# Attention and a residual MLP on one core: the first weight kept on chip for four batches, and the second product of batches 0 and 1 moved behind that of 2 and 3

## The chip, the core and the metric

The kernel runs on one core of one Trainium2 chip. The metric is the device time of one execution in microseconds (us); lower is better. The kernel before the change takes 743.62 us, the median of three runs (743.61 to 744.68).

The core's engines are named as in the profile: PE (matrix products), PEld (its weight loads, beside PE), DVE (vector work), ACT (functions such as the exponential and ReLU), POOL (a small general engine that here mostly issues DMAs), SP (which only issues DMAs). Each engine executes its own instructions in the order in which the program puts them; a DMA issued from POOL or SP also waits in that order.

## The reference

```python
def reference(q, k, v, alpha1, beta1, w_tok, alpha2, beta2, w_ch1, w_ch2, lam):
    # q (8, 16, 384, 64); k, v (8, 4, 384, 64): four query heads share a key head
    s = q @ k.T / 8                                  # per head
    a = exp(s - max(s)); a = a / sum(a)
    x = concat_heads(a @ v)                          # (8, 384, 1024)
    u = x + lam * (w_tok @ (alpha1 * x + beta1))     # mixes the 384 tokens
    a2 = alpha2 * u + beta2
    h = relu(a2 @ w_ch1)                             # w_ch1 (1024, 4096): "W1"
    return u + lam * (h @ w_ch2)                     # w_ch2 (4096, 1024): "W2"
```

All inputs and the output are float32 in DRAM. The kernel computes in bf16 and gathers in float32.

## The kernel before

**Two parts for each batch.** The *side work* of a batch (function `side`, L230) is the attention, the token mixing and the turned `a2`. Its sixteen heads go in eight pairs `p`. A pair takes score products (L280), the exponentials on ACT (L289), the product with v and the row sums (`av_piece`, L307; four DVE instructions at L325, L328, L333, L335), the token product (`tok`, L341; two DVE instructions at L352, L356), a store of `u` into `out` from SP (`spill`, L243) and a turn of `a2` (a DMA transpose from SP, L367, or for a few pairs PE and ACT, `turn`, L429). The *main work* is `h = relu(a2 @ W1)` and `h @ W2`.

**Main work of batches 0 and 1** (`main`, L526). W1 is cut into 16 chunks of 256 columns (512 KB in bf16). A chunk is read with a cast by a POOL DMA (L185) into one of six slots (`RING`) and given up after use; batch 1 takes the chunks in the opposite order and reuses the last six. A chunk makes two tiles of h, each eight matmuls of 384 columns (L537; 385 for batch 0, whose extra column gives the bias `bias1`) and one ReLU, on ACT (L546) or DVE (L548). Four tiles of batch 0 are made early, at the end of batch 0's side work. W2 lies whole in `arena` (sixteen POOL loads, L189). The second product is six groups (`ch`, L575) of 32 matmuls of 512 columns for each batch. Each group is multiplied by `lam` on DVE and stored by SP (batch 0) or added into `out` by a POOL DMA (batch 1).

**Main work of batches 2 to 7** goes in pairs of batches (`pair`, L661). Both products use a scheme with seven products of half-size blocks in place of eight. The first product (L707) reads `opb` blocks (sums of turned `a2`, L591 to L593) and sums of W1 chunks (L626, L631), and writes five hidden blocks `hid[:, t, 0..4]`, which are derived from the four ReLU outputs; `hid` lies in `arena`. The second product (`C`, L757) is 7 x 3 x 16 = 336 matmuls of 512 columns per pair. Its right-hand operands are seven sets of W2 sums, made once by DVE from the raw W2 (`sum_w2`, L601), written by SP to the DRAM tiles `w2s`, and fetched by SP for every pair, 28 chunks of 512 KB, through the same six slots (`fetch`, L636). One `queue` (L653) gives each freed slot its next transfer.

**Order.** The program writes out the order by hand. `main` and `pair` are generators that yield after a few matmuls; a table `plan` tells which side work, loads and sums are emitted after which yield ("step"). Batch 1's side work lies in the second product of batch 0, batch 2's in the first product of batch 1, batch 3's in the second product of batch 1, and those of 4 and 5 together in the second product of the pair 2 and 3, and so on.

**Three small things that the change touches.** The vectors `lam`, `alpha1`, `beta1`, `alpha2` must lie on all partitions: SP loads rows of them (`load_row_set`, L886) and a DVE shuffle spreads them (`to_all`, L891). The PSUM banks of batch 0's side work (`lead_banks`) are given up and taken over by three double banks (`threes`). Exponentials can be put into a list `late` and emitted later.

Of the kernel before, what the change touches and what calls it, by code (L numbers as in the profile page):

```python
# [12 lines left out]
def kernel(  # L13
# [63 lines left out]
    w2 = arena.rearrange("p (t h d) -> p t h d", t=NH, h=2)  # L77
# [34 lines left out]
    w2s = [tc.dram_tile([P, NDT * CW * P], bf, name=f"w2s{i}") for i in range(SLOTS)]  # L112
    PLACE2 = {o: i for i, o in enumerate((1, 2, 6, 5, 3, 7, 4))}
# [4 lines left out]
    def row(nt):  # L118
        return nt % NH, nt // NH
# [61 lines left out]
    w1_slots, w1_free = {}, list(range(RING))  # L181

    def load_w1(c):
        w1_slots[c] = w1_free.pop(0)
        nc.gpsimd.dma_start(out=w1[:, w1_slots[c]], in_=w1src[:, :, c * CW * P:(c + 1) * CW * P])  # L185

    def load_w2(dw, r, h):
        cs = slice(dw * 512, (dw + 1) * 512)
        nc.gpsimd.dma_start(out=w2[:, 4 * r:4 * r + 4, h, cs], in_=w2src[:, h * NH + 4 * r:h * NH + 4 * r + 4, cs])  # L189
# [15 lines left out]

    def tp_ps(shape, tag="tp"):
        return bank(shape, tag, "tp", bf)

    late, exps = [], [0]
# [8 lines left out]
    def h_part(nts, dts):  # L218
        for nt in nts:
            if nt % 2 == 0 and nt not in early:  # L220
                t = bank([P, 2, 512], "sc", "h")
                early[nt], early[nt + 1] = t[:, 0], t[:, 1]
            for dt in dts:
                nc.tensor.matmul(out=early[nt][:, :S + 1], lhsT=w1[:, w1_slots[nt // CW], dt, nt % CW * P:(nt % CW + 1) * P],
                                 rhs=a2Ts[0][:, dt, :S + 1], start=(dt == 0), stop=(dt == NDT - 1))
# [4 lines left out]
    def side(b):  # L230
# [21 lines left out]
        def k_transpose(h0, n=2, tag="tp"):  # L252
            ps = tp_ps([P, n * NST, P], tag)
# [6 lines left out]
        def q_transpose(p, n=2, tag="tp", eng="DVE"):  # L260
# [3 lines left out]
            ps = bank([P, n * NST, P], tag, "tp", src.dtype)  # L264
# [7 lines left out]
        def scores(i, later=False):  # L272
# [11 lines left out]
            def exp():  # L284
# [6 lines left out]
                exps[0] = 0 if first else 2  # L291

            if later:
                late.append(exp)
            else:
                exp()
# [44 lines left out]
        def tok(p):  # L341
# [13 lines left out]
            a2s[p] = next_a2() if b > NPL + 1 else sb.tile([P, NST, P], bf, tag="a2", name="a2", bufs=2)  # L355
# [54 lines left out]
        def av(p):  # L410
            av_piece(p, 0)
            av_piece(p, 1)
            while late:
                late.pop(0)()
# [11 lines left out]
        def by_pe(p):  # L426
            return b % 2 and p >= (NP - 3 if b > NPL else NP - 1)

        def turn(p):  # L429
            ps = three()[:, 0].rearrange("p a b -> p (a b)").bitcast(bf)[:, :S].rearrange("p (a b) -> p a b", a=NST)  # L430
# [5 lines left out]
        if not first:  # L436


            turns = {}
            if b == 1:  # L440
                turns = {4: [(to_all, 3, 0, 0), (to_all, 3, 1, 1), (load_row_set, 1, 1, 0), (load_row_set, 2, 0, 1)],
                         8: [(k_transpose, 0)], 12: [(to_all, 1, 0, 2), (to_all, 1, 1, 0), (load_row_set, 2, 1, 0)],
                         16: [(scale_beta,)], 20: [(to_all, 2, 0, 1), (to_all, 2, 1, 0)],
                         24: [(q_transpose, 0, 2, "av")], 28: [(k_transpose, 2)]}
                for i in range(3):
                    turns[32 + 4 * i] = [(q_transpose, 2 + 2 * i, 2, "av")]
            if (b - NPL) // 2 > 0:
# [4 lines left out]

                for j in range(9):
                    put(4 * j, scores2, j)
                for p in range(NP):
                    put(4 * (p + 1) + 3, av, p)
                    put(4 * (p + 1) + 6, tok, p)
                    put(4 * (p + 1) + 8, flip, p)
                    if by_pe(p):
                        put(4 * (p + 1) + 8 + (p == NP - 3), turn, p)  # L460
                return turns, at
            return turns, {
# [5 lines left out]
                **{39 + 4 * i - i // 2 * 2: [(turn, p)] for i, p in enumerate((5, 6, 7)) if by_pe(p)}}  # L468
# [50 lines left out]
    def store(b, ms, dw, o):  # L519
        at = by_tok(out[b])[:, ms, dw * 512:(dw + 1) * 512]  # L520
        if b:
            nc.gpsimd.dma_start(out=at, in_=o, accum_op=ADD)  # L522
        else:
            nc.sync.dma_start(out=at, in_=o)

    def main(b):  # L526
# [3 lines left out]
        seq = order1[::-1 if b % 2 else 1]  # L530
        for i, c in enumerate(seq):
            for j in range(CW):
# [3 lines left out]
                for dt in range(0 if begun else NDT):  # L536
                    nc.tensor.matmul(out=ps[:, :n], lhsT=w1[:, w1_slots[c], dt, j * P:(j + 1) * P],  # L537
                                     rhs=a2T[:, dt, :n], start=(dt == 0), stop=(dt == NDT - 1))
                    if dt == 3:
                        yield 0  # L540
# [3 lines left out]
                exps[0] -= 1  # L544
                if nt % 2 == 0 and exps[0] < 0:
# [4 lines left out]
                yield 0  # L550
            if i + RING < NCH:
                w1_free.append(w1_slots.pop(c))
                load_w1(seq[i + RING])

            if b == 0 and i == NCH - RING:
                for dw, r, h in [(0, 1, 1)] + [(0, r, h) for r in (2, 3) for h in range(2)] + [
                        (1, r, h) for r in range(4) for h in range(2)]:
                    load_w2(dw, r, h)
                load_next(2)
        nts = [c * CW + j for c in seq for j in range(CW)]  # L560
        units = [(dw, ms) for dw in range(NDW) for ms in range(NST)]
        runs = [(k, 0, NNT) for k in range(len(units))]
        if b == 0:
            most = 3 * NNT // 4
            runs[:2] = [(k, lo, hi) for lo, hi in ((0, most), (most, NNT)) for k in range(2)]
        open_ps = {}
        for k, lo, hi in runs:
            dw, ms = units[k]
            cs = slice(dw * 512, (dw + 1) * 512)
            if lo == 0:  # L570
                open_ps[k] = bank([P, 512], "mm", "ch")
            ps = open_ps[k]
            for i in range(lo, hi):
                nt = nts[i]
                nc.tensor.matmul(out=ps, lhsT=hT[:, nt, ms * P:(ms + 1) * P],  # L575
                                 rhs=w2[:, row(nt)[0], row(nt)[1], cs], start=(i == 0), stop=(i == NNT - 1))
                if i % 4 == 3 and i < NNT - 1:
                    yield 1
            if hi < NNT:
                continue  # L580
            o = obuf[:, k % 2 * 512:(k % 2 + 1) * 512]
            nc.vector.tensor_tensor(out=o, in0=ps, in1=lam_t[:, cs], op=MUL)
            if b == 0:
                nc.vector.tensor_tensor(out=o, in0=o, in1=xs[0][:, ms, cs], op=ADD)
            store(b, ms, dw, o)
            yield 1
# [14 lines left out]
    def sum_w2(r, o, i=0):  # L601

        def get(m):
            return w2[:, 2 * r:2 * r + 2, int(m[0] == "2"), (m[1] == "2") * 512:(m[1] == "2") * 512 + 512]
# [17 lines left out]
    def sum_w1(g, o):  # L622
        a, c = w1[:, w1_slots[g]], w1[:, w1_slots[g + NCH // 2]]
# [9 lines left out]
    NB = (B - NPL) // 2  # L633
# [11 lines left out]
    def free(slot):  # L645
# [3 lines left out]
        if queue:  # L649
            f, *a = queue.pop(0)  # L650
            f(*a)

    queue = [m for i in range(NB) for m in [(load_w1, c) for c in order1[2 if i else RING:]]  # L653
             + [(fetch, i, n) for n in range(SLOTS - 2 if i + 1 < NB else SLOTS)] + [(load_w1, c) for c in order1[:2] if i + 1 < NB]]

# [365 lines left out]
```

## Time and profile before

| | |
|---|---|
| median of three runs | 743.62 us |
| the profiled execution | 745.27 us |
| its span, first to last instruction | 743.5 us |
| PE busy | 731.1 us, 98% of the span |
| DVE busy | 514.6 us, 69% |
| ACT busy | 319.3 us, 43% |
| DMA packets that POOL issued (software queue) | 65.8% of 16 engines' span |
| DMA packets that SP issued (hardware queue) | 42.3% |

The profile is one execution. A group of instructions is shown as: line, engine, operation, output <- inputs, shape, count | busy time, mean ns of one | idle time of the engine just before them and what ended it. The mean of a matmul is its latency; matmuls overlap, so busy time over count is nearer to what one takes. A table of windows gives the busy time of each engine in a stretch of the span, the number of instructions in brackets, then the granted PE clock, the DMA share and GB/s.

### The profile page before, as it was taken

The page shows a single profiled execution, that of the slowest core. Times are in us where ns is not written, and L with a number is a line of the kernel's source. Part 1 is how long each engine was busy: PE and PEld are TensorE (multiplying, and loading weights), DVE is VectorE, ACT ScalarE, POOL GpSimd, SP SyncE. Part 2 cuts the span into 40 slices and gives each one's busy share as a digit, 9 for nine tenths or more (in the row PEclk, how much of TensorE's full clock was granted, in tenths as well). Part 3 has the DMA queues.
Part 4 walks back from the last instruction along what each step waited for, and adds up shares of the span by engine and source line. Part 5 has one row for each costly group of instructions (what it writes and reads, how often), then busy time and mean ns, then how long its engine had stood idle before and what let it go on. Part 6 is the DMA issues. An engine that isn't in the chain of part 4 may idle for free.

```text
span 743.5 us, 14441 instructions
## 1 busy us (share of the span) xinstructions
PE 731.1 (98%) x5708; PEld 416.1 (56%) x5769; DVE 514.6 (69%) x998; ACT 319.3 (43%) x458; POOL 163.4 (22%) x211
## 2 busy tenths in 40 slices
PE   8999999999999999999999999999999999999997
PEld 5866555566555566645555566655555566654444
DVE  7763366567687889748778977747957987762354
ACT  7632431334332566653443366664334166660000
POOL 9434220420000232201003433210002331000011
PEclk9999999999999999999999999999999999999999
DMA  9999999999998999999979999998988998935976
GB/s 185 194 201 200 207 219 168 172 184 204 221 275 243 178 222 214 256 219 213 272 246 205 200 174 174 173 216 181 246 278 221 183 165 115 162 117 176 291 210 158
DMA packets 218017, 151.32 MB, mean 204 GB/s; under 512 B 88660, under 2 KB 197060, under 8 KB 217948
## 3 DMA queue, kind: packets, MB, share of 16 engines
q0 software_dynamic: 120304, 64.60, 65.8%
q1 hardware_dynamic: 97100, 85.39, 42.3%
q8 instruction: 45, 0.74, 0.4%
q10 hardware_dynamic: 544, 0.39, 0.2%
q14 instruction: 24, 0.20, 0.1%
HBM read 154.84 MB, written 38.27 MB: 260 GB/s over the span
## 4 chain that ended last, share of the span: by engine, by line
PE 85%; DMA 8%; POOL 2%; issue 2%; DVE 2%; POOLq 0%; DVEq 0%
PE C L757 29%; PE X L707 17%; PE Y L707 8%; PE ch L575 8%; PE h L537 7%; PE Z L707 4%; PE sc L280 4%; PE sc L345 3%; DMA ops<-a 3%; DMA w<-in_moe_w_ch_dram 2%; PE one L320 2%; DMA q_raw<-in_q_dram 2%; PE sc L320 1%; POOL w L185 1%; DMA rows<-in_moe_lam_dram 1%
## 5 line engine op out<-in xcount | busy, mean ns | idle before, releaser
L757 PE MATMUL C<-w,arena 128*128 128x512 bf16 (+2 forms) x949 | 219.9, 372 | 2.3
L289 ACT ACTIVATE es<-sc 128x1024 bf16<-128x1024 f32 x126 | 121.8, 1022 | 162.7 <-PE sc L280 158.6
L757 PEld LDWEIGHTS <-arena 128*128 128x128 bf16 x1040 | 93.7, 98 | 99.8 <-issue 7.6
L712 ACT ACTIVATE hT<-X,bias 128x384 f32<-128x384 f32 x144 | 83.7, 581 | 67.4 <-PE X L707 60.4
L707 PEld LDWEIGHTS <-w 128*128 128x128 bf16 x768 | 75.1, 98 | 50.3 <-issue 0.4
L185 POOL DMA_DIRECT2D w<-in_moe_w_ch_dram x68 | 62.4, 924 | 128.9 <-PE X L707 68.2
L575 PE MATMUL ch<-arena,hT 128*128 128x512 bf16 x366 | 87.9, 379 | 1.0 <-issue 0.3
L522 POOL DMA_DIRECT2D out_dram<-hT x33 | 29.3, 887 | 261.5 <-DVE hT L677 135.7
L537 PE MATMUL h<-ops,w 128*128 128x384 bf16 (+1 forms) x480 | 83.7, 327 | 1.9 <-DVE hT L548 0.9
L707 PEld LDWEIGHTS <-pad 128*128 128x128 bf16 x576 | 56.4, 98 | 37.2
L707 PE MATMUL X<-ops,w 128*128 128x384 bf16 x384 | 70.5, 326 | 0.0
L707 PE MATMUL X<-ops,pad 128*128 128x384 bf16 x384 | 70.3, 326 | 0.0
L537 PEld LDWEIGHTS <-w 128*128 128x128 bf16 x480 | 45.1, 98 | 32.3 <-issue 2.8
L575 PEld LDWEIGHTS <-hT 128*128 128x128 bf16 x384 | 34.7, 98 | 36.8 <-issue 2.5
L352 DVE TENSOR_TENSOR xr<-sc,xr 128x384 f32<-128x384 f32 x56 | 31.1, 555 | 34.1 <-PE sc L345 34.1
L320 PEld LDWEIGHTS <-es 128*128 128x128 bf16 x1008 | 38.3, 97 | 12.4
L280 PE MATMUL sc<-qT,kT 64*128 64x384 bf16 (+2 forms) x576 | 43.8, 272 | 0.9 <-DVE xr L328 0.2
L345 PEld LDWEIGHTS <-wtokT 128*128 128x128 bf16 x576 | 37.4, 98 | 12.9 <-DVE a L335 2.7
L707 PE MATMUL Z<-ops,w 128*128 128x384 bf16 x192 | 39.1, 326 | 0.0
L707 PE MATMUL Y<-ops,w 128*128 128x384 bf16 x192 | 39.1, 326 | 0.0
L714 DVE TENSOR_TENSOR arena<-Y,hT 128x384 bf16<-128x384 f32 x48 | 26.8, 558 | 17.3 <-ACT hT L712 15.0
L345 PE MATMUL sc<-a,wtokT 128*128 128x128 bf16 x504 | 37.3, 219 | 0.1
(140 smaller groups left out, 858.2 us busy)
## 6 DMA issues: line engine op xcount, KB each, us to landing
w<-w2s SPq DMA_DIRECT2D x80, 512.0 KB, 4.7
w<-in_moe_w_ch_dram POOLq DMA_DIRECT2D x68, 512.0 KB, 9.9
out_dram<-xr SPq DMA_DIRECT2D x56, 192.0 KB, 5.6
out_dram<-hT POOLq DMA_DIRECT2D x33, 256.0 KB, 6.9
arena<-in_moe_w_ch_dram POOLq DMA_DIRECT2D x16, 512.0 KB, 19.8
w2s<-arena SPq DMA_DIRECT2D x28, 256.0 KB, 3.5
q_raw<-in_q_dram POOLq DMA_DIRECT2D x28, 192.0 KB, 10.4
w2s<-pad SPq DMA_DIRECT2D x16, 256.0 KB, 2.7
```

The lines of the kernel that those rows point to most:

```text
L185: nc.gpsimd.dma_start(out=w1[:, w1_slots[c]], in_=w1src[:, :, c * CW * P:(c + 1) * CW * P])
L280: nc.tensor.matmul(out=sc[:, hh, k % 4:k % 4 + n], lhsT=kT[r, 2 * p // G, BLK[hh][sk], :], rhs=qT[r, p, st:st + n, :], start=True, stop=True)
L289: nc.scalar.activation(out=e, in_=sc, func=EXP, scale=scale_qk)
L320: nc.tensor.matmul(out=av[:, hh, sq, :], lhsT=ess[k // 4][:, m % 2, k % 4, :], rhs=vb[:, sk, hk, :], start=(sk == 0), stop=(sk == NST - 1))
L345: nc.tensor.matmul(out=ps[:, tt, :], lhsT=wtokT[:, st, tt * P:(tt + 1) * P], rhs=a1s[p][:, st, :], start=(st == 0), stop=(st == NST - 1 an ...
L352: nc.vector.tensor_tensor(out=u, in0=ps, in1=u, op=ADD)
L522: nc.gpsimd.dma_start(out=at, in_=o, accum_op=ADD)
L537: nc.tensor.matmul(out=ps[:, :n], lhsT=w1[:, w1_slots[c], dt, j * P:(j + 1) * P], rhs=a2T[:, dt, :n], start=(dt == 0), stop=(dt == NDT - 1))
L575: nc.tensor.matmul(out=ps, lhsT=hT[:, nt, ms * P:(ms + 1) * P], rhs=w2[:, row(nt)[0], row(nt)[1], cs], start=(i == 0), stop=(i == NNT - 1))
L707: nc.tensor.matmul(out=ps, lhsT=tb[g, o][:, dt, e * P:(e + 1) * P], rhs=opb(LEFT1[o])[:, dt], start=(o in (1, 2, 7) and dt == 0), stop=(dt ...
L712: nc.scalar.activation(out=snap[o, e], in_=ps, func=IDENT, bias=hi if o == 5 else lo)
L757: nc.tensor.matmul(out=x, lhsT=hid[:, t, LEFT2[o], ms * P:(ms + 1) * P], rhs=rhs[:, t % 4 * 512 + c0:t % 4 * 512 + c1], start=(o in (1, 6, ...
```

## The change

1. **W1 stays.** The 16 chunks are loaded once, 14 of them into regions of `arena`, two into slots of `w1`. Batch 0, batch 1 and the first product of the pair 2 and 3 read them from there.
2. **h goes to DRAM.** Each chunk's two tiles of h of batches 0 and 1 are written by SP to the DRAM tiles `hs` (196,608 bytes a chunk). `main` ends there: it has no second product.
3. **The second product of batches 0 and 1** is a run of the seven-product scheme, `second(1, 0)`, behind that of the pair 2 and 3, `second(0, 2)`. Four reads of 1.57 MB bring the halves of h back into `hid`, three during `second(0, 2)` and one in the first steps of `second(1, 0)`. Eight DVE sums make the derived blocks. It fetches the 28 `w2s` chunks again and adds into `out`, where batch 0's `u` has been stored as a whole before.
4. **W2** is no longer held. Raw pieces (r = 0 to 7, two loads each) come into ring slots or two regions, and their sums are made in `main(0)` (r = 0), `main(1)` (1 to 3) and the first product of 2 and 3 (4 to 7).
5. **The side work moves.** Batch 1's lies in the first product of batch 0; those of 2 and 3 both in the first product of batch 1; batch 4's in `second(0, 2)`, batch 5's in `second(1, 0)`; 6 and 7 as before. In `main(1)` ACT makes 24 of 32 ReLUs (before: 9) and DVE 8. At most one late exponential is emitted per step.
6. **The start of `main(0)`:** the first two `to_all` come at step 0, before any ReLU of `main` (before: at the fourth matmul step, behind the ReLUs of the four early tiles); `threes` takes over the banks at step 4 and the first turn of batch 1's keys is put there. The rows for `to_all` lie in ring slots 4 and 5.

The core of the diff, as the new order and the new parts:

```diff
-    def load_w1(c):
-        w1_slots[c] = w1_free.pop(0)
+    def load_w1(c, keep=False):
+        g, second = c % (NCH // 2), c // (NCH // 2)
+        w1_slots[c] = (second if g == NCH // 2 - 1 else None) if keep else w1_free.pop(0)
+        slot = w1_slots[c]
+        w1_at[c] = w1[:, slot] if slot is not None else region(2 * g + 2 + second).rearrange("p (a c) -> p a c", a=NDT)
...
     def main(b):
+        def put_by(c):
+            nc.sync.dma_start(out=hs[b][:, c * CW:(c + 1) * CW], in_=hT[:, c * CW:(c + 1) * CW])
...
-                if nt % 2 == 0 and exps[0] < 0:
+                if nt % (4 if b else 2) != 1:
                     nc.scalar.activation(out=hT[:, nt, :], in_=ps[:, :S], func=RELU, bias=c1)
...
-                nc.tensor.matmul(out=ps, lhsT=hT[:, nt, ms * P:(ms + 1) * P],
-                                 rhs=w2[:, row(nt)[0], row(nt)[1], cs], start=(i == 0), stop=(i == NNT - 1))
...
+        def back(k, b, h):
+            nc.sync.dma_start(out=hid[:, :, k], in_=hs[b][:, h * NH:(h + 1) * NH])
...
+                    if again and o == 1 and h and ms:
+                        for r in (0, 1) if ms == 1 else (2, 3):
+                            ts = slice(4 * r, 4 * r + 4)
+                            tt(out=hid[:, ts, 3], in0=hid[:, ts, 2], in1=hid[:, ts, 1], op=ADD)
...
+                    if again and o == 1 and h == 0 and ms == 1:
+                        back(1, 1, 1)
+                    if i == 0 and h and ms == 0 and o in (5, 7, 4):
+                        back(*{5: (0, 0, 0), 7: (4, 0, 1), 4: (2, 1, 0)}[o])
...
+        put(0, 0, to_all, 3, 0, 0)
+        put(0, 0, to_all, 3, 1, 1)
+        put(0, 0, load_row_set, 1, 1, 0)
+        put(0, 0, load_row_set, 2, 0, 1)
+        for c in order1[9:]:
+            put(0, 0, load_w1, c, True)
+        put(0, 1, lambda: nc.sync.dma_start(out=by_tok(out[0]), in_=xs[0]))
...
+        for u, f, h in ((4, k_turn, 0), (5, q_turn, 0), (6, q_turn, 2), (20, k_turn, 2), (22, q_turn, 4), (24, q_turn, 6)):
+            put(0, u, f, h, 2)
+        put_all(0, at, lambda u: 9 + int(1.12 * u))
+        put(0, 26, load_next, 2)
+        for r in range(3):
+            put(0, 27 + r, load_w2, r)
+        put_flips(0, 2, range(47, 57, 2))
+        put_w2(0, 0, (52, 54, 56, 58))
...
+        put_w2(1, 1, (3, 6, 9, 12))
+        put_w2(2, 1, (14, 17, 20, 23))
...
+        put_all(1, side(2)[0], lambda u: int(0.7 * u))
...
+        put_w2(3, 1, (30, 34, 38, 42))
+        put_all(1, side(3)[0], lambda u: 32 + int(0.68 * u))
...
+        put_sums(1, (62, 62, 63, 63))
...
+        phases = (main(0), main(1), first_product(0), second(0, 2), second(1, 0), first_product(1), second(2, 4),
+                  first_product(2), second(3, 6))
+        for ph, steps in enumerate(phases):
+            for u, _ in enumerate(steps):
+                if (ph, u) == (0, 4):
                     lead_banks.close()
                     threes.append(side_banks.enter_context(tc.psum_pool(name="threes", bufs=3)))
+                for f, *a in plan.pop((ph, u), []):
                     f(*a)
+                if late:
+                    late.pop(0)()
```

`first_product` and `second` are the two halves of the old `pair`; `by_pe` turns one pair of batch 5 on PE instead of three.

## The prediction

> **What bounds the kernel now.** I read the engine shares first. PE is busy 731.1 of 743.5 us, so a change pays only if it takes matmuls off PE or idle time out of the 12.4 us left. The chain of work that ended last agrees (85% PE), and so does its list in order of time, where the last second product is one block of matmuls:
>
> ```profile
> PE 731.1 (98%) x5708; PEld 416.1 (56%) x5769; DVE 514.6 (69%) x998; ACT 319.3 (43%) x458; POOL 163.4 (22%) x211
> ...
> PE 85%; DMA 8%; POOL 2%; issue 2%; DVE 2%; POOLq 0%; DVEq 0%
> ...
> L575 PE MATMUL ch<-arena,hT 128*128 128x512 bf16 x366 | 87.9, 379 | 1.0 <-issue 0.3
> ```
>
> ```profile
> 699.53 10.74 PE C L757 x49
> ```
>
> So 49 matmuls of 512 columns take 10.74 us, 0.219 us each (the 379 ns is a latency). Next the windows by stage: first and second product of batch 0 (36.3, 77), of batch 1 (133, 190), the first pair's two (244, 318).
>
> ```profile
> core 0: us, PE busy (x) PEld busy (x) DVE busy (x) ACT busy (x) POOL busy (x), PEclk, DMA share, GB/s
> ...
> 36.30:77.00 40.70, 40.38 (x276) 24.59 (x275) 20.70 (x51) 11.87 (x33) 16.18 (x20) 1.00 1.38 201
> 77.00:133.00 56.00, 55.09 (x479) 29.74 (x486) 31.14 (x60) 18.35 (x20) 10.37 (x14) 1.00 1.30 198
> 133.00:190.00 57.00, 55.31 (x537) 35.22 (x539) 39.46 (x76) 21.53 (x27) 13.94 (x17) 1.00 1.27 188
> 190.00:244.00 54.00, 53.38 (x474) 29.26 (x477) 38.34 (x78) 18.78 (x21) 4.32 (x5) 1.00 0.93 247
> ...
> 318.00:419.00 101.00, 100.10 (x902) 53.37 (x919) 74.03 (x146) 37.86 (x42) 13.29 (x15) 1.00 1.03 229
> ```
>
> From 36.3 to 244, which the change rewrites, PE idles 0.32 + 0.91 + 1.69 + 0.62 = 3.5 us, and DVE is loaded to 51 to 71%.
>
> **What goes.** (1) The plain second products of batches 0 and 1 are 2 x 6 x 32 = 384 matmuls; a seven-product run is 336. The program's instruction lists agree: 48 matmuls of 512 columns fewer. 48 x 0.219 = **10.5 us**. (2) Batch 5 turns one pair on PE, not three: 6 matmuls of 18 that take 2.0 us, **0.7 us**. (3) 20 of 68 W1 loads go. Loads end no PE wait of note today (0.3 us), so this is worth nothing itself.
>
> **What comes: the start of `main(0)`.** In DVE's order the two row shuffles now stand ahead of the four early tiles' ReLUs. Before, DVE's timeline was:
>
> ```profile
> 37.16 0.62 DVE L548 TENSOR_SCALAR hT<-h,bias 128x384 bf16<-128x384 f32 x1
> 37.70 0.15 DVE L543 COPY bias<-h 128x1 f32<-128x1 f32 x1
> 37.88 0.62 DVE L548 TENSOR_SCALAR hT<-h,bias 128x384 bf16<-128x384 f32 x1
> 38.84 0.01 DVE L892 LOAD_MASK_SELECT vecs<-rows  x1 [0.34 <-DMA rows<-in_moe_lam_dram]
> 38.87 0.73 DVE L892 STREAM_SHUFFLE vecs<-rows 128x512 f32<-128x512 f32 x1
> ```
>
> The rows land at 38.8, and nothing makes them earlier: the POOL loads and clears ahead of them are as many and as large. So the ReLUs start after the shuffles, at 40.1, and the second ends at about 41.7 (bias and ReLU, twice 0.8). The first key turn of batch 1, now at step 4 on PE, takes banks that the early tiles held; in the changed program it waits for the DVE count that this second ReLU raises. PE ended the early tiles at 36.2 and has four matmuls (0.8 us) before that turn: it stands from 37.1 to 41.7, **4.6 us**. Bounds: 0.3 us (what PE lost to these ReLUs before) if the rows come early, 5.5 if they come a microsecond later.
>
> **The clock after that wait.** The last rows of the windows show what idling does to the granted clock (PE's last matmul ends at 739.5):
>
> ```profile
> 739.50:741.00 1.50, 0.00 (x0) 0.00 (x0) 1.21 (x4) 0.00 (x0) 0.00 (x0) 1.00 0.45 175
> 741.00:742.00 1.00, 0.00 (x0) 0.00 (x0) 0.00 (x0) 0.00 (x0) 0.00 (x0) 1.00 0.76 262
> 742.00:743.50 1.50, 0.00 (x0) 0.00 (x0) 0.00 (x0) 0.00 (x0) 0.00 (x0) 0.51 0.01 5
> ```
>
> After 2.5 us without a matmul the clock is still 1.00, then 0.51. The wait is 4.6 us, so PE may resume at half clock. The price from a row: the 13 warm-up matmuls at the kernel's start average 465 ns against 327 for the same shape warm, 1.8 us in all. Bounds 0 and 1.8; I take the middle, **0.9 us**.
>
> The Trainium skill, "TensorE: Matmul & The Clock Gate", Part 1, says that an idle window of about 3.4 us halves the clock and that about 3.4 us of activity restores it. This speaks against the change, and the tail agrees with its first half. As an estimate from that page the term would be half of 3.4, 1.7 us, and the forecast below 0.8 higher.
>
> **The rest of `main(0)`.** DVE's work there: 16 ReLUs (0.62) with biases (0.16), 12.4; batch 1's side work, 8 x (0.19 + 5 x 0.558) = 23.8; six shuffles 4.3; key and query copies 3.3; four W2 sums 2.7; 1.2 for `scale_beta`: 48 us. PE has 224 x 0.166 (60 h matmuls in 9.97 us) = 37 plus about 13 for the side work ((100.1 - 336 x 0.219) / 2) and 4 for turns: 54. So DVE has room. The first W2 sum waits for a POOL load that stands behind nine loads of k, q and v and seven of W1; POOL's queue before moved 512 KB per 2.55 us (issues at 73.16, 75.74, 78.26, each released by a landing), and SP now also writes h. By that rate the load lands at about 85, and the sum is due at 86 plus the wait above. Cost 0, at most 3. If late, DVE's ReLUs wait behind the sum, and PE behind them after two tiles. I take before's idle of 36 to 133, **1.2 us**. The h stores sit in SP's queue ahead of spills and turns, one per chunk with its ReLU a chunk old: nothing.
>
> **`main(1)`, two batches' side work over one first product.** DVE: 2 x 23.8 = 47.7; 8 ReLUs 4.9; 12 W2 sums of 0.685, 8.2; four W1 sums 2.7; 12 `sums_a` of 0.354, 4.2: **67.7 us**. PE: 256 x 0.163 (16 in 2.61 us) = 41.8 plus 2 x 13.3: **68.3**. ACT: 36 x 1.02 + 24 x 0.58 + 2, 53: no bound. DVE goes to 99% of PE's time, from 70%. The row nearest to that is the densest 10 us of batch 1:
>
> ```profile
> 180.00:190.00 10.00, 9.30 (x87) 5.99 (x88) 9.61 (x19) 1.16 (x2) 0.00 (x0) 1.00 0.94 204
> ```
>
> At 96% DVE, PE lost 0.7 of 10 us: 68.3 x 0.07 = **4.8 us**. What is late: a pair's `av` on DVE holds its `tok` on PE; the spill of three pairs earlier must have landed before DVE reuses `xr` (some 6 us after its issue now, 5.6 to land); and the last `sums_a` now stand at the final two steps, while the pair's third product needs them 1.3 us into the next stage. Lower bound 0 (the sums fit, 67.7 < 68.3). Upper: DVE's waits for PE in 133 to 244 stay as they were (5.4 + 1.1 and 7.5 + 2.9): 67.7 + 16.9 - 68.3 = 16.3.
>
> **The two second products.** Each has one batch's side work where one had two, and the fetches are the same 28 per run. Three reads of h are issued 20 us or more before use. The fourth has about 6 us (24 matmuls and some side work) before DVE's first sum waits on it; 512 KB took 4.7 us to land, this is 1.57 MB, so 4.7 to 14.1. DVE's side chain stands behind that wait, PE's `tok` behind the chain with about 3 us of slack: 0 to 5.5; I take **0.5**. The eight sums (0.95 each, 7.6 us) fit: DVE there has 74 - 24 + 8 = 58 of 87 us. Twelve additions into `out` on POOL have no load behind them in that stage. All later stages stay.
>
> **Sum**, against the profiled execution: -10.5 - 0.7 - 3.5 (old idle) + 4.6 + 0.9 + 1.2 + 4.8 + 0.5 = **-2.7 us**, span 743.5 to 740.8. That execution took 745.27 us, 1.65 above the median; on the median of 743.62, **740.9 us**.
>
> **Rivals.**
> - *The waits are covered.* Rows early and DVE packing without loss: 4.6, 0.9 and 4.8 fall to 0.3, 0 and 1: -2.7 - 9.0, **731.9 us**; half of it, 736.4 us. For: DVE ran 87% in 244 to 318 with PE idle 0.05 us. Against: the shuffles' place in the order.
> - *DVE becomes the bound of `main(1)`* (the slower side): one mechanism, DVE's in-order queue, priced by its waits, 4.8 to 16.3 us. No gain is left at 4.8 + 2.7 = 7.5 us; slower by over 0.2% from 9.0 on. At 14, **750.1 us**. For: 99% load, spills landing as xr is due. Against: the two dense rows seen.
> - *It nearly cancels*: the waits come to 6 to 9 us and the gain to nothing, **743 us**.
> - *The saving isn't there*: no, the count of matmuls is in the program; what can fail is that PE's freed time is spent waiting, which is the two rivals above.
>
> **Chances.** A measurement tells 0.2% (1.5 us) from no change. Forecast (735.5 to 742.1) 0.44, covered (below 735.5) 0.14, cancels 0.19, DVE-bound and slower 0.23. So faster 0.58, same 0.19, slower 0.23. The range 733 to 748.5 leaves out some 0.07 below and 0.12 above. Within the forecast alone: 735.5 to 742.1.
>
> **What would show it.** After's windows: second products of 88 us instead of 101 (right if within 1); a PE gap near 37 to 42, with the row shuffles ahead of the early ReLUs and a clock below 1.00 behind it; `main(1)` with DVE over 90% and PE idle of 4 to 6 us, released by DVE. Wrong if PE waits for W1, W2 or h from DRAM for more than 3 us, or if `main(1)` idles over 9 us.

## The result, and the profile after

The changed kernel takes **827.85 us**, the median of four runs (823.2 to 831.02), beside 744.12 us for the kernel before on the same chip (743.61 to 744.68): 1.112 times as long, with a 95% interval of 1.1054 to 1.1186. The forecast was 740.9 us. The profiled execution took 825.09 us, its span is 823.3 us. Medians in this document leave out a run more than 1.5% above the fastest of its kernel, which counts as slow; that takes two runs each from e1, e6 and e8 and one from e12.

The page of the changed kernel, first the engine shares, then PE and its granted clock in 40 slices, then the chain that ended last:

```profile
PE 744.6 (90%) x5667; PEld 417.5 (51%) x5715; DVE 526.5 (64%) x1008; ACT 327.5 (40%) x474; POOL 150.3 (18%) x197
...
PE   8785958579899999998669999999999999999998
...
PEclk9996989789999999999779999999999999999999
...
PE 72%; DMA 16%; DVE 5%; POOL 2%; issue 2%; SPq 1%; ACT 1%; DVEq 0%; POOLq 0%
```

PE idles 78.7 us where it idled 12.4, and DMA has 16% of the chain where it had 8%. PE is busy 13.5 us longer with fewer matmuls, because some run below full clock: in the two stages that gain length, PE's busy time in each us of the trace, times what the granted clock there lacks of 1.00, comes to some 20 us (an estimate). The slices give the places: the deep dips lie in the second to ninth slice (20 to 185 us) and in the nineteenth to twenty-first (370 to 432 us). The two stages are those that the change rewrote. `main(0)` and `main(1)` are over at 224.9 us; by the prediction's own terms (36.3, then 54 + 6.7 and 68.3 + 4.8) it should have been 170. `second(0)` and `second(1)` take 201.0 us together (297.9 to 498.9), not 2 x 88. These two make 80 of the 82.5 us by which the span misses the forecast; the first product between them takes 73.1 us (before: 72.8), and what follows 324.4 (before: 324.6).

The windows of the changed kernel (columns as in the prediction):

```profile
core 0: us, PE busy (x) PEld busy (x) DVE busy (x) ACT busy (x) POOL busy (x), PEclk, DMA share, GB/s
...
60.00:80.00 20.00, 8.57 (x74) 5.25 (x75) 6.72 (x16) 3.59 (x5) 3.14 (x6) 0.66 0.83 140
...
100.00:120.00 20.00, 11.56 (x106) 7.16 (x104) 10.48 (x22) 3.44 (x8) 1.48 (x2) 0.83 1.10 182
...
140.00:160.00 20.00, 9.16 (x105) 5.47 (x106) 8.80 (x18) 7.29 (x10) 1.40 (x2) 0.78 1.41 215
160.00:180.00 20.00, 14.32 (x142) 9.31 (x141) 10.88 (x23) 5.10 (x7) 0.00 (x0) 0.84 0.82 221
...
380.00:400.00 20.00, 10.24 (x38) 3.66 (x37) 4.15 (x6) 1.94 (x2) 2.54 (x3) 0.76 1.11 263
```

Where PE is idle in the end of `main(0)` and in `main(1)`, which begins near 121 us, DVE is busy 44 to 54% of the time, not over 90% as forecast. Both wait. PE's waits name DVE, and only DVE's own waits tell for what, so the two lists are read together. PE's waits from 36 to 225 us come first (total, number, longest), DVE's in the same stretch second:

```profile
PE h L539 <- DVE hT L549: 16.8, 5, 11.8
PE sc L354 <- DVE a L344: 12.1, 4, 6.4
PE sc L290 <- DVE xr L337: 10.9, 3, 10.0
PE sc L266 <- DVE hT L549: 5.2, 1, 5.2
```

```profile
DVE xr L337 <- DMA out_dram<-xr: 20.6, 6, 7.4
DVE pad L587 <- DMA w2s<-pad: 13.9, 4, 5.5
DVE vecs L874 <- DMA w<-in_moe_alpha_dram: 12.6, 1, 12.6
```

DVE stands for spills, stores of W2 sums and a row load that have not landed; ReLUs and attention sums queue behind it in its order, and PE stands for those. The loads of W2 are not in DVE's list: it comes to the first W2 sum only at 116.2 us, when its load is there.

The row load is a wait that nobody wrote. The sixth row goes into the tile `w1` on every 32nd partition. The last two W1 loads go into the same tile. They share no byte, but the row load waits until a W1 load has landed, and so does everything behind it on SP:

```profile
SPq L870 <- DMA w<-in_moe_w_ch_dram: 25.4, 1, 25.4
```

The start of `main(0)` is as forecast: the shuffles run at 39.18, the second early ReLU at 41.32, and PE stands 5.19 us (forecast 4.6):

```profile
41.99 0.71 PE L266 MATMUL sc<-ident,k 128*128 128x128 bf16 x6 [5.19 <-DVE hT L549]
```

The chain in order of time at the turn from `second(0)` to `second(1)` shows fetches of W2 sums that land late, a fetch held on SP (`SPq L610`), and the fourth read of h, for which DVE stands longest:

```profile
374.78 8.74 DMA w<-w2s
...
397.62 6.94 SPq L610
...
405.09 11.81 DMA arena<-hs
```

```profile
DVE arena L664 <- DMA arena<-hs: 25.8, 1, 25.8
```

### The profile page after: what moved, and what is told of

Its sections match the earlier page's. It is cut to its first block, busy times and chain, and to the rows that moved or that the text cites. A ratio compares the mean times of both kernels' runs of the same rounds, so it can differ in the third digit from the quotient of the medians.

```text
span 823.3 us, 14488 instructions
## 1 busy us (share of the span) xinstructions
PE 744.6 (90%) x5667; PEld 417.5 (51%) x5715; DVE 526.5 (64%) x1008; ACT 327.5 (40%) x474; POOL 150.3 (18%) x197
## 4 chain that ended last, share of the span: by engine, by line
PE 72%; DMA 16%; DVE 5%; POOL 2%; issue 2%; SPq 1%; ACT 1%; DVEq 0%; POOLq 0%
PE C L684 33%; PE X L746 15%; PE Y L746 8%; DMA out_dram<-xr 6%; PE h L539 4%; PE Z L746 4%; PE sc L290 3%; DMA w<-in_moe_w_ch_dram 3%; PE sc L354 3%; PE one L329 2%; DMA w<-w2s 2%; DMA arena<-in_moe_w_ch_dram 2%; DMA w2s<-pad 1%; DMA arena<-hs 1%; SPq L610 1%
## 5 line engine op out<-in xcount | busy, mean ns | idle before, releaser
L684 PE MATMUL C<-w,arena 128*128 128x512 bf16 (+1 forms) x1281 | 298.2, 379 | 12.6 <-DMA w<-w2s 9.8
L684 PEld LDWEIGHTS <-arena 128*128 128x128 bf16 x1376 | 128.0, 99 | 154.5 <-issue 19.9
L539 PE MATMUL h<-ops,arena 128*128 128x384 bf16 (+1 forms) x416 | 86.0, 348 | 15.1 <-DVE hT L549 14.8
L746 PEld LDWEIGHTS <-w 128*128 128x128 bf16 x544 | 53.2, 98 | 35.6 <-issue 0.2
L539 PEld LDWEIGHTS <-arena 128*128 128x128 bf16 x416 | 39.0, 103 | 42.6 <-issue 13.2
L746 PE MATMUL X<-ops,w 128*128 128x384 bf16 x272 | 49.9, 326 | 0.0
L190 POOL DMA_DIRECT2D w<-in_moe_w_ch_dram x34 | 31.6, 933 | 72.7 <-PE X L746 59.2
L290 PEld LDWEIGHTS <-kT 64*128 64x128 bf16 x576 | 21.1, 96 | 41.1 <-issue 23.8
L712 DVE TENSOR_TENSOR hT<-C,hT 128x512 f32<-128x512 f32 (+2 forms) x34 | 22.8, 672 | 29.6 <-PE C L684 29.3
L746 PE MATMUL Y<-ops,pad 128*128 128x384 bf16 x192 | 35.1, 326 | 0.0
L547 ACT ACTIVATE hT<-h,bias 128x384 bf16<-128x384 f32 x40 | 23.2, 581 | 29.8 <-PE h L539 26.9
```

The source lines that it names most:

```text
L190: nc.gpsimd.dma_start(out=w1_at[c], in_=w1src[:, :, c * CW * P:(c + 1) * CW * P])
L290: nc.tensor.matmul(out=sc[:, hh, k % 4:k % 4 + n], lhsT=kT[r, 2 * p // G, BLK[hh][sk], :], rhs=qT[r, p, st:st + n, :], start=True, stop=True)
L539: nc.tensor.matmul(out=ps[:, :n], lhsT=w1_at[c][:, dt, j * P:(j + 1) * P], rhs=a2T[:, dt, :n], start=(dt == 0), stop=(dt == NDT - 1))
L684: nc.tensor.matmul(out=x, lhsT=hid[:, t, LEFT2[o], ms * P:(ms + 1) * P], rhs=rhs[:, t % 4 * 512 + c0:t % 4 * 512 + c1], start=(o in (1, 6, ...
L746: nc.tensor.matmul(out=ps, lhsT=tb[g, o][:, dt, e * P:(e + 1) * P], rhs=opb(LEFT1[o])[:, dt], start=(o in (1, 2, 7) and dt == 0), stop=(dt ...
```

## The experiments

Four theories were held against each other (VectorE, TensorE and ScalarE are DVE, PE and ACT). **A**: DMAs that were asked for too late, or stand behind others in SP's or DVE's order, land late. Its parts are A1 (spills) and A2 (W2's loads and stores). **B**, the prediction's: VectorE's own work bounds `main(1)`. **C**: the DMA engines cannot move the bytes. **D**: the transposes that SP issues hold SP. All kernels from e3 to e17 carry the edit of e2. Each kernel ran four times; the stages are from one profiled run each. Four kernels with the same `main(0)` and `main(1)` (e2, e8, e10, e12) end it at 217.3 to 225.1, and three later ones that are alike there (e11, e13, e14) at 184.8 to 189.1. So a `main` moved by less than some 8 us, or some 4 in the later kernels, is not told from nothing.

| kernel | median us (range of all four) | main(1) over | second(0) + second(1) |
|---|---|---|---|
| the change | 827.9 (823.2 to 831.0) | 224.9 | 201.0 |
| e1_rows | 816.8 (813.7 to 826.3) | 216.9 | 203.8 |
| e2_rows_start | 827.9 (819.2 to 831.0) | 222.8 | 203.5 |
| e3_no_h | 785.6 (783.2 to 790.6) | 206.9 | 184.4 |
| e4_buffers | 819.9 (814.3 to 824.0) | 223.6 | 200.5 |
| e5_no_w2 | 787.4 (784.5 to 789.4) | 182.4 | 203.7 |
| e6_no_spill | 806.0 (801.6 to 823.7) | 198.8 | 203.5 |
| e7_pe_turns | 811.3 (807.6 to 814.5) | 211.8 | 203.0 |
| e8_back_act | 824.5 (821.9 to 836.0) | 217.3 | 205.2 |
| e9_w2_later | 809.6 (804.9 to 810.5) | 204.3 | 201.5 |
| e10_back_quarter | 816.1 (814.1 to 817.6) | 220.1 | 196.2 |
| e11_all_main | 792.3 (789.3 to 793.9) | 188.0 | 205.8 |
| e12_back_pieces | 811.2 (810.5 to 823.0) | 225.1 | 193.9 |
| e13_both | 778.7 (777.9 to 782.9) | 189.1 | 191.1 |
| e14_flips_between | 773.2 (772.6 to 773.9) | 184.8 | 189.3 |
| e15_mended_no_h | 761.7 (760.8 to 764.9) | 181.6 | 184.0 |
| e16_pe_flips | 770.7 (769.3 to 773.1) | 183.2 | 187.2 |
| e17_sp_turns | 782.9 (778.6 to 785.4) | 197.2 | 186.2 |
| e18_rows_as_changed | 790.4 (789.2 to 791.3) | 201.7 | 188.5 |

### The start of main(0): e1_rows, e2_rows_start

```diff
-        for c in order1[9:]:
+        for c in order1[9:14]:
             put(0, 0, load_w1, c, True)
...
         put(0, 10, load_row_set, 2, 1, 2)
+        for c in order1[14:]:
+            put(0, 11, load_w1, c, True)
```

> The changed kernel, with the loads of the last two W1 pieces (the ones that go into the w1 tile) issued behind the sixth row load instead of ahead of it. Theory A (late landings and SP's order): the sixth row load no longer waits 25.4 us for W1, so the row shuffle's wait of 12.6 us, PE's wait of 11.8 us behind it and the clock of 0.66 in 60 to 80 us go, and what stands behind that load on SP is 25 us earlier; 805 to 815 us, with idle of PE left between 95 and 180 us and between 375 and 420 us. Theory B (VectorE's own work bounds main(1), as the prediction had it): the 12 us and the half clock go here as well, 810 to 815, and VectorE shows no long waits in main(1). If the row load is only named by the trace and something else held it: 825 or more.

e2 also moves these from step 0 to step 5:

```diff
-        put(0, 0, to_all, 3, 0, 0)
+        put(0, 5, to_all, 3, 0, 0)
```

> As e1_rows, and the two shuffles of the lambda row, with the two row loads behind them, moved from the first step of main(0) to its sixth, behind the early ReLUs. The prediction's first step said that PE stands 4.6 us there: 4 to 7 us less than e1_rows (the half clock after the stand included), and no idle of PE between 36 and 60 us. If the early ReLUs are held by something else than the shuffles, as e1_rows within 1 us.

The long stand went in both, as A said: PE is busy 19.4 (e1) and 19.8 (e2) of 20 us in 60 to 80, at clock 1.00. The first stand, 4.7 us in e1, is 1.4 in e2. The time did not follow. e1's median is 11 us lower, by two runs (813.7 and 820.0); its two others (826.3) lie among the change's. e2 gained nothing at all. PE reached the next missing transfer earlier and stood there longer; e2's DVE waits in 36 to 225 us are

```profile
DVE pad L587 <- DMA w2s<-pad: 23.9, 3, 14.1
DVE pad L587 <- DMA w<-in_moe_w_ch_dram: 18.3, 2, 17.2
```

The first W2 sum, at the end of `main(0)`, waits for its load, and later sums wait for stores. A's sizes failed, because it added up waits that take each other's place.

### What lies behind: e3_no_h, e4_buffers

```diff
-            if i:
-                put_by(order1[i - 1])
-        put_by(order1[-1])
...
-                        back(1, 1, 1)
...
-                        back(*{5: (0, 0, 0), 7: (4, 0, 1), 4: (2, 1, 0)}[o])
```

> As e2_rows_start, but without the stores of h of batches 0 and 1 and without the four reads of it: the second product of batches 0 and 1 is computed from whatever the tile holds, so their output is not the reference's; every product is still computed. Theory A: the waits for w2s in second(0) and second(1) (9.8 us), the sum's wait for h, the tok waits and the half clock there go, and the SP queue of main(0) and main(1) has 32 transfers of 192 KB less: 30 to 50 us less than e2_rows_start. Theory B: only the part between 375 and 420 us goes, about 20 us, and main(1) is as long as before. Theory C (bytes: the DMA engines are full): as theory A, and e4_buffers gains nothing.

e4 gives the outputs that wait for their spill more places:

```diff
-                xr[p] = sb.tile([P, NST, P], f32, tag="xr", name="xr", bufs=3)
+                xr[p] = next_xr(b)
...
+    def next_xr(b):
+        xr_turn[0] += 1
+        i = (xr_turn[0] - 1) % 7 - 3
+        if b > 3 or i < 0:
+            return sb.tile([P, NST, P], f32, tag="xr", name="xr", bufs=3)
+        more = arena if b == 3 else pad
+        return more.bitcast(f32)[:, i * S:(i + 1) * S].rearrange("p (a d) -> p a d", a=NST)
```

> As e2_rows_start, with seven places instead of three for the attention outputs that wait for their spill to land (four more in parts of tiles that are idle then), for batches 1 to 3. Same instructions, same bytes. Theory A: VectorE's 20.6 us of waits for spills to land go, and with them most of PE's idle time behind them between 95 and 180 us: 15 to 30 us less than e2_rows_start. Theory B (VectorE's work) and theory C (the DMA engines are full): no change, within 3 us.

e3 gives 42.3 us, 19.1 of it at the second products and 15.9 in `main`. e4's 8 us are not told from nothing, as the ranges overlap: DVE now waits for the W2 sums' stores (33.3 us) and loads (19.2). So more room at one of several late transfers is worth little by itself; alone, this looked like C.

### One suspect at a time: e5_no_w2, e6_no_spill, e7_pe_turns, e8_back_act

```diff
-        put_w2(0, 0, (52, 54, 56, 58))
...
-        put_w2(1, 1, (3, 6, 9, 12))
-        put_w2(2, 1, (14, 17, 20, 23))
...
-        nc.sync.dma_start(out=at, in_=w2s[n])
+        nc.sync.dma_start(out=at, in_=w2s[n | 2])
```

> As e2_rows_start, but without the first half of W2's sums: the eight loads, sixteen sums and twenty-eight stores of it that lie in main(0) and main(1) are left out, and the fetches read the other half's stores twice, so the second products of all batches are wrong in those terms; the matmuls and fetches are all there. Theory A2 (the W2 work put into main(0) and main(1) is what the stalls come from: VectorE, in its order, stands for a W2 load or a w2s store that has not landed, and PE's ReLUs and sums stand behind it): most of the idle of PE between 80 and 180 us goes, 30 to 45 us less than e2_rows_start, main(1) over at 185 us or before. Theory B (VectorE's own work): its 0.69 us a sum are 11 us of work; up to 11 us less. Theory D (transposes on SP): under 10 us less, SP's transposes still take 5 us and more.

```diff
-            if not first:
+            if b > 3:
                 spill(p)
```

> As e2_rows_start, but without the stores of the attention outputs of batches 1 to 3 (24 of 192 KB in main(0) and main(1)): the output of these batches lacks that term. Theory A1 (the spills' landings hold VectorE): the waits for them go and 15 to 30 us with them. Theory A2 or D: they go, but the waits for w2s stores, W2 loads and transposes take their place, as with the seven buffers of e4_buffers: 3 to 10 us less than e2_rows_start.

```diff
-            return p >= {1: NP - 1, 3: NP - 3, 5: NP - 1, 7: NP - 3}.get(b, NP)
+            return p >= {1: 0, 2: 0, 3: 0, 5: NP - 1, 7: NP - 3}.get(b, NP)
```

> As e2_rows_start, with the 20 transposes of batches 1 to 3 in main(0) and main(1) that SP issued made by TensorE instead (some 0.3 us each, 6 us of PE, and a copy on ScalarE); the transposes of k and q stay on SP. Theory D (a transpose that SP issues while the loads are queued holds SP 5 to 9 us, and all that is behind it): PE's idle time between 80 and 180 us falls by 15 to 30 us, 10 to 25 us less than e2_rows_start. Theory A2: the stand for the W2 load stays, under 8 us less, or slower.

```diff
-            nc.sync.dma_start(out=hid[:, :, k], in_=hs[b][:, h * NH:(h + 1) * NH])
+            nc.scalar.dma_start(out=hid[:, :, k], in_=hs[b][:, h * NH:(h + 1) * NH])
```

> As e2_rows_start, with the four reads of h issued on ScalarE's DMA queue instead of SP's. Same bytes at about the same times. Theory A (order: the fetches of w2s stand behind the 1.5 MB reads in SP's queue): the waits for w2s go, the stretch from 375 to 430 us loses half its idle time or more, 8 to 20 us less than e2_rows_start. Theory C (bytes: 6 MB of h in some 45 us on top of fetches and stores is more than the DMA engines move): within 3 us of e2_rows_start.

e5 settles B. It takes 11 us of DVE work away and ends `main(1)` 40.4 us earlier, so some 29 us of that were waits for W2's transfers, or for others that these held up. e6 gives 24 us in `main`, more than A2 allowed for it, but in the fastest of its four runs; e7 gives 11, and 16.6 in time, the size that D named. In `main`, e3, e5, e6 and e7 add up to 91 us, where 55 are lost: each takes away something that the rest waits behind, so no one of these gains is a share of the loss. e8 gains nothing that can be told: another issuing engine is no second way out. The Trainium skill, "DMA: Bandwidth & Descriptors", "Issuing engines are not separate DMA queues", says so: DMAs from all engines interleave on the same sixteen DMA engines, and only issue time is saved. The 205.2 us of e8 against 203.5 of e2 agree.

### Order or bytes: e9_w2_later, e10_back_quarter, e11_all_main, e12_back_pieces

```diff
-        put_w2(0, 0, (52, 54, 56, 58))
...
+        for r in range(3):
+            put_w2(r, 1, tuple(12 * r + u for u in (6, 9, 12, 15)))
...
-            v = (spare((5, 6, 4).index(o)) if pairs else part(3 + (4 * r + (5, 6, 7, 4).index(o)) % 3)).rearrange("p (a c) -> p a c", a=2)
+            v = (spare((5, 6, 4).index(o)) if pairs else part((4 * r + (5, 6, 7, 4).index(o)) % 6 if r < 3 else 3 + (5, 6, 7, 4).index(o) % 3)).rearrange("p (a c) -> p a c", a=2)
```

> As e2_rows_start, with the first half of W2's sums later and with more places: none in main(0), the sixteen sums spread over steps 6 to 55 of main(1), six places instead of three for the sums of the first three rows, the loads of W2 12 steps apart. Same bytes, same instructions. Theory A2 in its order form (VectorE stands for a load or a store that was asked for too shortly before): most of e5_no_w2's gain of 40 us comes without leaving anything out, 25 to 40 us less than e2_rows_start, and the 18 us stand for W2 near 90 us is gone. Theory C (bytes: the DMA engines move no more in that time): under 10 us, with the waits moved to other landings.

```diff
-            nc.sync.dma_start(out=hid[:, :, k], in_=hs[b][:, h * NH:(h + 1) * NH])
+            nc.sync.dma_start(out=hid[:, :4, k], in_=hs[b][:, h * NH:h * NH + 4])
```

> As e2_rows_start, but each of the four reads of h brings only the first 4 of its 16 blocks (0.4 MB instead of 1.6), at the same places in the order; the second product of batches 0 and 1 is computed from a partly stale tile, so their output isn't the reference's. Theory C (bytes): second(0) and second(1), 203.5 us together in e2_rows_start and 184.4 in e3_no_h, fall to 184 to 190. Theory A (one long transfer's place in SP's order and VectorE's wait for it, whatever its size): 195 or more.

e11 is e9 with e7's edit and e4's (eight places, in two regions of `arena`).

> As e9_w2_later, with TensorE's transposes of e7_pe_turns and with eight places for the attention outputs that wait for their spill. If the stalls of main(0) and main(1) are matters of order and of places, the three gains add up to main(1) over at 185 us or before and 785 us or less. If they share one limit (bytes), it is within 5 us of the better of e7_pe_turns and e9_w2_later.

```diff
+                    if again and o == 1 and r < 4:
+                        back(1, 1, 1, r)
+                    if i == 0 and r < 4 and o in (5, 7, 4):
+                        back(*{5: (0, 0, 0), 7: (4, 0, 1), 4: (2, 1, 0)}[o], r)
```

> As e2_rows_start, with each of the four reads of h cut into four, begun half a product earlier and issued a sixth of a product apart, and with the sums that need the fourth read put one product later in VectorE's order. Same bytes. Theory A (order): second(0) and second(1) fall from 203.5 us to 184 to 192, 12 to 20 us less than e2_rows_start. Theory C (bytes): 198 or more.

e9 gives 18.3 us, between A's 25 to 40 and C's under 10; DVE's stand for the W2 load is gone, and PE's longest wait is now one of 15.2 us for a q that SP transposes. e9 and e7's 16.6 make 34.9, and e11 gives 35.6 (with e4's 8 it would be 43). It ends `main(1)` at 188.0, where A said 185, and its 792.3 us miss A's 785. That e9 ends `main(1)` 18.5 us earlier with the same bytes shows that order counts; that later W2 loads also spread the bytes over more time is part of what "order" means here. C isn't out for the rest: e7's edit takes 20 transposes off the DMA engines as well as off SP's queue, and no run parts the two. At the second products a quarter of the bytes (e10) gains 7.3 us and whole reads in quarters (e12) 9.6, half of what e3 gained there. e10's 196.2 is what A said (195 or more); e12's 193.9 lies between A's 192 and C's 198. So there too the order counts, and not that of the reads alone.

### Adding up, and what is left: e13 to e18

e13 is e11 and e12. e14 moves the transposes of batch 5:

```diff
-                n = 7 if b < 6 else 4
+                n = {4: 5, 5: 7}.get(b, 4)
...
-        put_flips(3, 5, range(62, 72, 2))
+        put_flips(3, 5, range(49, 59, 2))
```

> e11_all_main and e12_back_pieces together, all of the computation in it. If the losses of main and of the second products are separate matters, they add up: 778 to 784 us. If the fetches at the turn from second(0) to second(1) are held by something else than the reads of h, second(0) and second(1) stay at 192 us or more.

> As e13_both, with the five transposes of k and q of batch 5, which SP issues at steps 62 to 70 of second(0), moved to steps 49 to 57, between the second and third read of h, and batch 4's attention drawn together from 7 steps a piece to 5 so that the tiles are free by then. Theory D (transposes that SP issues into a full queue take 5 to 7 us each and hold the fetches behind them): the wait for w2s at the turn falls under 5 us, second(0) and second(1) to 178 to 186 us, 6 to 12 us less than e13_both. If the stores or the reads themselves hold the fetches: within 3 us of e13_both.

e15 takes the stores and the reads of h out of e14:

```diff
-            if i:
-                put_by(order1[i - 1])
-        put_by(order1[-1])
...
-                        back(1, 1, 1, r)
...
-                        back(*{5: (0, 0, 0), 7: (4, 0, 1), 4: (2, 1, 0)}[o], r)
```

> As e14_flips_between, without the stores and reads of h (the output of batches 0 and 1 is then not the reference's). What it is less than e14_flips_between is what the round trip of h costs when the order around it is mended: by theory A (order) under 12 us, by theory C (bytes) 25 us or more, as between e2_rows_start and e3_no_h (42 us).

e16, on e14:

```diff
-        put_flips(0, 2, range(47, 57, 2))
+        side2, k_turn, q_turn = side(2)
+        for u, f, h in ((49, k_turn, 0), (50, q_turn, 0), (52, q_turn, 2), (54, k_turn, 2), (56, q_turn, 4), (58, q_turn, 6)):
+            put(0, u, f, h, 2)
```

> As e14_flips_between, with the k and q of batch 2 turned by TensorE at the end of main(0) (36 matmuls of 128 columns, six copies on VectorE) instead of by five transposes on SP. Theory D: the waits for qT and kT (10 us in e11_all_main) go, main(1) is over 4 to 10 us earlier. Theory B (VectorE's work, six copies more): not earlier, or later.

e17 is e16 without e7's edit, e18 is e16 without e2's.

> As e16_pe_flips (770.7 us), with the transposes of the attention outputs of batches 1 to 3 back on SP: 20 of TensorE's 72-matmul groups and 20 copies on ScalarE go, some 7 us of PE. If SP's transposes are slow only among bursts of loads, and these are now spread: 1.2 to 3 us each, main(1) over at 176 to 182 us, 763 to 769 us. If they are slow by what is in their own queue: 5 us and more each near 100 us again, main(1) over at 186 us or later, 774 or more.

> As e16_pe_flips, with the row loads, the shuffles and the last two W1 loads back where the change put them. The stands of 5 and 12 us at 37 to 70 us come back. If each stall is its own loss, and e1_rows and e2_rows_start gained nothing only because the next stall took it up: 784 to 795 us, 14 to 24 us more. If the stands are covered by something else even now: within 4 us of 770.7.

e13 adds up (778.7). e14 gains 5.5 us, just under the 6 to 12 that D said; but its two second products take 1.8 us less (189.3, where D said 178 to 186), and the rest lies in `main(1)`, which its edit doesn't touch. So e14 does not show D. e15 prices the round trip of h: 11.5 us when the order is mended, against 42.3 when it was not (A said under 12). e16 ends `main(1)` 1.6 us earlier, which isn't told from nothing, not 4 to 10; its median gains 2.5. From its page, the engine shares, PE and the granted clock:

```profile
PE 735.7 (96%) x5763; PEld 417.9 (54%) x5811; DVE 529.4 (69%) x1014; ACT 335.9 (44%) x494; POOL 150.3 (20%) x197
...
PE   8999988989999999979899999999999999999997
...
PEclk9999999999999999998999999999999999999999
```

The deep dips before 200 us are gone: from 36.3 to 183.2 us PE idles 14.4 us, where it idled 50.5 to the end of `main(1)` in the change, and the granted clock is 1.00 throughout. e16 is the best kernel with all of the computation: 1.0357 times the kernel before (1.0332 to 1.0382). It gives back 57 of the change's 84 us and does not beat the kernel before.

e17 corrects D. SP's transposes now hold SP for 1.2 to 4.9 us each, and the kernel is 12.1 us slower all the same: the time that D's branch named (774 or more), without its holds of 5 us and more. What is late is the landing; from e17's chain:

```profile
90.25 19.41 DMA ops<-obuf
```

PE waits 9.8 us for that turned block at the start of `main(1)`. e17 also shows what order and places do without that help: with all transposes but five back on SP, `main(1)` is over at 197.2, 25.6 us before e2. e18 settles e1 and e2: the same two stands (3.9 and 11.8 us of PE), put back into the mended kernel, cost 19.7 us, the half clock behind them included. They were never free; a larger wait behind them took up what their cure gave.

## Why the prediction was wrong

- **The saving of 10.5 us.** It is there: outside its waits the second stage costs what was forecast. e15's two second products take 184.0 us, of which PE idles 7.7; the remaining 176.3 is the forecast's 2 x 88.
- **The start, 4.6 us, and the clock, 0.9.** The first is right: 5.19 by the same row. The clock fell to 0.50 as PE resumed and stayed there for 3.4 us of matmuls, which costs half of that, 1.7 (an estimate), near the upper bound of 1.8. But the term counted one fall; the later stands bring more, some 20 us in all by the estimate above.
- **"The h stores sit in SP's queue ... nothing", and the first W2 sum "cost 0, at most 3".** The first failed while the other landings are late: without the stores `main` is 15.9 us shorter (e3 against e2); when the order is mended it is 3.2 (e15 against e14), not told from nothing. The second holds in the change only because DVE comes late to that sum; with the row stands cured (e2) it waits 17.2 us there. The prediction put the landing of that load at about 85 us, by a rate of 512 KB per 2.55 us between issues on POOL. In the change the first four loads of W2 are issued from 82.8 us on and take 16.6 us to land at the median, in e2 25.6. And DVE's wait for the stores of the W2 sums, whose places are used again, is in no term: 13.9 us in the change, 23.9 in e2. The prediction took the landing times as rows of their own. In that stretch nearly all the DMA engines' time is taken, in the kernel before (each digit is a fortieth of the stretch, in tenths):

```profile
DMA  9999999999999999999999999999999999991979
...
DMA packets 18518, 9.85 MB, mean 197 GB/s; under 512 B 10856, under 2 KB 18002, under 8 KB 18514
...
arena<-in_moe_w_ch_dram POOLq DMA_DIRECT2D x2, 512.0 KB, 24.4
```

and in e2_rows_start:

```profile
DMA  9999999999899999489999999999998999999999
...
DMA packets 15382, 8.92 MB, mean 178 GB/s; under 512 B 10781, under 2 KB 13586, under 8 KB 15378
...
w<-in_moe_w_ch_dram POOLq DMA_DIRECT2D x4, 512.0 KB, 25.6
```

  In the kernel before a load took as long to land, and more bytes moved. No engine waited for it there. In e2 DVE is at the sum before the load is there, with the ReLUs behind it in its order.
- **`main(1)`, 4.8 us, priced by DVE's load.** This is the step that failed most: DVE's work was priced, and not what DVE waits for. In the rewritten stretch it stood 20.6 us for spills. A median of 5.6 us was taken for a spill to land; the chain of the change has one of 16.1 and one of 16.9, and DVE is about half idle there. The rival "DVE becomes the bound" named DVE's in-order queue and "spills landing as xr is due", but bounded it by the kernel before's waits, 16.3 us, in which nobody had waited for a landing. With the landings mended (e16), `main(1)` is over at 183.2, 13 us after the forecast's 170; 9.6 of these are PE's added turns (72 matmuls of 7.9 us where 12 took 1.3, and 36 more, of 3.0).
- **The sixth row load.** It is in no term. The prediction followed the start of `main(0)` through POOL's and DVE's order, and not SP's wait for two other DMAs into the same tile: 11.8 us of PE, and 17 to 20 us with the first stand and the clock behind them (e18).
- **The fourth read, 0.5 us.** DVE waited 25.8 us for it and PE 7.8 behind that, with 9.8 more for fetches. It took 11.8 us to land, within the 4.7 to 14.1 that the prediction gave. What the term left out is SP's queue ahead of it: two transposes held SP for 13.1 us from 375.9 and two fetches for 10.8 from 394.2, so the read was issued only at 405.1, 14 us after DVE had come to the sum. The third, which the same sum needs and the prediction had issued 20 us or more before use, was issued at 393.7.
- **The condition** "wrong if PE waits for W1, W2 or h from DRAM for more than 3 us" was the right thing to look at; it should have been a rival with a price.

Open: in e16 PE still idles 9.7 us in the two second products, in e15 without any h 7.7, so neither h nor batch 5's transposes are all of it. How much of the 14 us of `main` between e17 and e16 is SP's order and how much the transposes' load on the DMA engines isn't shown either. And it isn't shown how much each of the 25 us of a load's landing owes to which other transfer.

## What to carry to other kernels

When an edit moves a transfer nearer to its use, price it by the lead between issue and use, against the longest landing of that kind among the traffic of that stage, not by its median and not by the engines' work. Ask of each in-order engine what stands behind an instruction that waits for a DMA, and of each load which other transfers share its tile. Cure stalls in one place and judge them together: a cured wait may return nothing until the next one is cured too.

## What the runs showed of the hardware

- **Half clock.** In the change, PE's last matmul before the long stand ends near 59.6 us; the granted clock is 1.00 to 62.5, then 0.50 until 76, and 1.00 from 77, although matmuls run again from 71.4. So it fell after some 3 us and came back after some 5 of work:

```profile
59.00:62.50 3.50, 0.60 (x19) 0.47 (x16) 0.00 (x0) 0.74 (x2) 1.50 (x2) 1.00 1.46 202
...
63.00:65.00 2.00, 0.00 (x0) 0.00 (x0) 0.00 (x0) 0.00 (x0) 0.00 (x0) 0.50 1.47 197
```

  Neither time is fixed. Behind the first stand the clock fell only near 42.2, 5.3 us after PE's last matmul, and came back after 3.6 us of work; at the end of the kernel before it fell after 2.5. The Trainium skill, "TensorE: Matmul & The Clock Gate", Part 1, gives about 3.4 us for both; the times measured here lie on both sides of it.
- **A transpose that SP issues** holds SP for 1.2 to 3.0 us from 80 to 125 us in the kernel before, and for up to 9.6 us there in e2, with six W2 loads issued just before and during it. What makes it longer isn't shown. The kernel before's SP in order of time (start, duration):

```profile
116.17 2.95 SPq L172 DMA_TRANSPOSE kT<-k  x1
```

The same of e2_rows_start:

```profile
90.26 9.63 SPq L178 DMA_TRANSPOSE qT<-q_raw  x1
101.07 6.63 SPq L376 DMA_TRANSPOSE ops<-obuf  x1
```
